# Three small reorderings in a tuned attention and GLU kernel: PSUM tiles of the last output, an earlier tanh, and LayerNorm work behind the output projection

## The chip, the cores and the metric

One core of a Trainium2 chip. The metric is the device time of one execution in microseconds (us). A profile of one execution of each kernel gives the start and end of every instruction; its span is about 1.7 us shorter than the device time. Some executions, over 1.5% above the fastest of their kernel, are marked slow (one of 43 of the kernel before in the rounds of e13: 258.73 us, the fastest 253.67); every ratio below uses fast runs alone, while the medians of rows that name slow runs include them. The kernel before takes 254.48 us (median of three, 254.15 to 256.01).

## The reference, cut to what matters

```python
mod = (silu(c) @ w_mod)            # sa, ca, ga, sb, cb, gb
h = layernorm(x) * (1 + ca) + sa
x = x + ga * A(h)                  # 16 heads of 28, 4 segments of 512 tokens:
                                   # softmax attention inside a segment (a_dot), and
                                   # phi(q) @ M / (phi(q) @ z) from the segments before (a_mem),
                                   # mixed by sigmoid(beta), then @ wo
h = layernorm(x) * (1 + cb) + sb
x = x + gb * B(h)                  # (sigmoid(h @ w_gate) * (h @ w_up)) @ w_down, F = 1792
```

x is 2048 x 448 in bf16. A causal mask acts inside a segment.

## The kernel before

Everything lies in SBUF. TensorE (PE) gets one long list of matmuls; a small clock in the program (`later`, `tick`) decides where the work of the other engines is put into their own lists. PSUM tiles of the tag "m" (q, k, v, `acc`, `mem`, `gps`, `ups`, `dps`, `pwo`) rotate through four buffers. VectorE (DVE) empties most of them, ScalarE (ACT) does exponentials and copies, GpSimd (POOL) masks and `rs`, SyncE (SP) issues transposes through the DMA.

```python
# conditioning: c arrives by DMA; PE multiplies silu(c) with w_mod
    th = const.tile([KP, NK], F32)
    nc.scalar.activation(th[:], c_col[:], AF.Tanh, scale=0.5)
# ... (after the weight loads were issued)
    for t in range(TPS):
        ln0.stats(t)
        if t % 2:
            ln0.rstd(t - 1, t + 1)
    silu_ops()                       # DVE: silu from th
    mod_cols(((1, 1),), warm[:, 2, :])   # PE

class LN:                            # cut
    def rstd(self, a, b):            # POOL: (var + eps) ** -0.5
    def norm(self, i):               # DVE: xn = (x - mean) * rs, and a small copy
    def norm_t(self, i):
        self.norm(i)
        nc.sync.dma_start_transpose(self.h[:, :, i*P:(i+1)*P], self.xn[:, i, :])   # hT, SP's queue
    def modulate(self, kc, vi):      # DVE, on hT

def phi(src, wait, tag, then=None):  # exp on ACT, then two DVE instructions (lines 369, 370)
def mem_read(s, hc):                 # PE: mem; DVE lines 478 to 482 read it and free its PSUM buffer
def pv(s, hc):                       # PE: acc; DVE lines 457 to 463 read it

def wo_fin(s, t):                    # after the Wo matmuls of token tile t
    nc.vector.tensor_tensor(xt, pw[:, 0:D], xt, ALU.add)
    ...
    ln.stats(t)
    ln.rstd(t, t + 1)
    later((2400, 2000, 2000, 1500)[s], lambda: ln.norm_t(t), ("ln2", s))
    # modulate follows once all four tiles are transposed; gate_up reads hT

def down(s, t):
    dp = m_f32("dps")
    ...
    n = 2 if i == NSEG * TPS - 1 else 1      # the very last tile goes in two halves
    for h in range(n):
        c = slice(h * D // n, (h + 1) * D // n)
        for fc in range(NFC):
            nc.tensor.matmul(dp[:, c], ...)
        nc.vector.tensor_tensor(ot[:, c], dp[:, c], x_sb[:, i, c], ALU.add)
        eng.dma_start(out_dram[...], ot[:, c])
```

The softmax here doesn't subtract the row's maximum and nothing guards it: scores larger than these inputs give would overflow.

Of the kernel before, what the change touches and what calls it, by code (L numbers as in the profile page):

```python
# [9 lines left out]
F32 = mybir.dt.float32  # L10
AF = mybir.ActivationFunctionType
# [6 lines left out]
def kernel(  # L18
# [16 lines left out]
    nc = tc.nc  # L35
# [4 lines left out]
    TPS = L // P  # L40
    F = B_w_gate.shape[1]
    NFC = F // P
    KP, NK = 112, 4
# [5 lines left out]
    scale = float(Dh) ** -0.5  # L49
# [10 lines left out]
    const = ctx.enter_context(tc.tile_pool(name="const", bufs=1))  # L60
# [6 lines left out]
    def m_f32(name):  # L67
        return ps_m.tile([P, 512], F32, tag="m", name=name)
# [7 lines left out]
    def later(ns, fn, tag):  # L76
        deferred.append((clock[0] + ns, len(deferred), fn, tag))
# [14 lines left out]
    def need(*tags):  # L92
        for tag in tags:
            late_ = [d for d in deferred if d[3] == tag]
            if late_:
                print("forced", tag, len(late_), max(d[0] for d in late_) - clock[0])
            run_deferred(lambda d: d[3] == tag)


    c_col = const.tile([KP, NK], BF16)  # L100
# [14 lines left out]
    def load_wm(engs, j):  # L115
        t = wm_bufs[j % 2]
        n = NK // len(engs)
        for i, eng in enumerate(engs):
            k = slice(i * n, (i + 1) * n)
            eng.dma_start(t[:, 0:NK * D].rearrange("p (k n) -> p k n", n=D)[:, k, :], wmod_k[:, k, j * D:(j + 1) * D])  # L120
        return t

    wm_bufs = [wts.tile([KP, NK * D + DP - D], BF16, name=f"wm{i}") for i in range(2)]
    wm = {j: load_wm((nc.sync, nc.scalar), j) for j in (1, 0)}
    wq_sb = wts.tile([P, NK, H, HP], BF16)
    wk_sb = wts.tile([P, NK, H, HP], BF16)
    wv_sb = wts.tile([P, NK, D], BF16)
# [64 lines left out]
    coef = const.tile([P, 2, H], F32)  # L192


    th = const.tile([KP, NK], F32)
    nc.scalar.activation(th[:], c_col[:], AF.Tanh, scale=0.5)
    silu = const.tile([KP, NK], BF16)

    def silu_ops():
        nc.vector.tensor_scalar(th[:], th[:], 0.5, 0.5, op0=ALU.mult, op1=ALU.add)  # L200
        nc.vector.tensor_tensor(silu[:], th[:], c_col[:], ALU.mult)
# [13 lines left out]
    def mod_cols(jobs, cp=None):  # L215
        evac = cp is None
        cp = cp_of[0] = m_f32("cp") if evac else cp
        for j, vi in jobs:
            for kc in range(NK):
                for k in range(NK):  # L220
                    c0 = k * D + kc * P
                    if vi >= 2 and kc == NK - 1:
                        for r in (0, LW):
                            nc.tensor.matmul(cp[r:r + LW, vi * NK + kc:vi * NK + kc + 1], lhsT=wm[j][:, c0:c0 + LW],
                                             rhs=silu[:, k:k + 1], start=(k == 0), stop=(k == NK - 1),
                                             tile_position=(0, r))
                        continue
                    nc.tensor.matmul(cp[:, vi * NK + kc:vi * NK + kc + 1], lhsT=wm[j][:, c0:c0 + P],
                                     rhs=silu[:, k:k + 1], start=(k == 0), stop=(k == NK - 1))
        if evac:  # L230
            mod_evac(jobs)
# [281 lines left out]
    def wo_tile(s, t):  # L513
        wo_mm(s, t, range(NK))
        wo_fin(s, t)

    def wo_fin(s, t):
        pw = pw_of.pop(t)
        xt = x_sb[:, s * TPS + t, :]
        nc.vector.tensor_tensor(xt, pw[:, 0:D], xt, ALU.add)  # L520
        if t == 0:
            ln2_of[s] = LN([x_sb[:, s * TPS + i, :] for i in range(TPS)], ("2", s))
        ln = ln2_of[s]
        ln.stats(t)
        ln.rstd(t, t + 1)
        later((2400, 2000, 2000, 1500)[s], lambda: ln.norm_t(t), ("ln2", s))
        if t == TPS - 1:
            for kc in range(NK):
                later(6500 + 400 * kc, lambda kc=kc: ln.modulate(kc, 2), ("ln2", s))
# [33 lines left out]

    def down(s, t):
        need("wd")
        dp = m_f32("dps")
        i = s * TPS + t
        ot = work.tile([P, D], BF16, tag="ot", bufs=2)
        eng = nc.scalar if s >= NSEG - 2 else nc.sync
        n = 2 if i == NSEG * TPS - 1 else 1  # L570
        for h in range(n):
            c = slice(h * D // n, (h + 1) * D // n)
            for fc in range(NFC):
                nc.tensor.matmul(dp[:, c], lhsT=fT_of[(s, fc)][:, t * P:(t + 1) * P], rhs=wd_sb[:, fc, c],  # L574
                                 start=(fc == 0), stop=(fc == NFC - 1))
            nc.vector.tensor_tensor(ot[:, c], dp[:, c], x_sb[:, i, c], ALU.add)  # L576
            eng.dma_start(out_dram[i * P:(i + 1) * P, c], ot[:, c])
# [27 lines left out]
    def down_jobs(s):  # L605
        return [(NFC * MV, lambda t=t: down(s, t)) for t in range(TPS)]
# [66 lines left out]
    for t in range(TPS):  # L673
        ln0.stats(t)
        if t % 2:
            ln0.rstd(t - 1, t + 1)
    silu_ops()
    mod_cols(((1, 1),), warm[:, 2, :])
    for t in range(2):
        ln0.norm(t)  # L680
# [155 lines left out]
    for t in range(TPS):  # L836
        wo_mm(last, t, range(NK - 1 if t < 2 else 0, NK))
        wo_fin(last, t)
        tick((200, 1400, 760, 760)[t])
# [34 lines left out]
```

## Time and profile before

| stretch | where | what PE waits for |
|---|---|---|
| head | 8.62 us | 1.22 us for `silu` |
| segment 0's LN2 | 76.42 us | 1.69 us at `acc`, for a PSUM buffer |
| same | 78.96 us | 0.63 us at the first gate/up, for `hT` |
| tail | 247.50 us | 0.48 us at the last half tile |
| whole | span 252.1 us | PE busy 96% |

In a timeline line the first number is the start and the second the length in us; the bracket at its end is how long the engine idled before it, and for whom. A group of several instructions (x4) is merged into one line. The slice row of the page shows the granted TensorE clock in tenths of full speed, in 40 slices of the span (9 is 90% or more):

```profile
PEclk9999999999999999999999999999999999999999
```

In this execution of the kernel before the clock never fell once it was up.

### The profile page before, as it was taken

How to read it: one execution, taken by the hardware profiler on the slowest of the kernel's cores; microseconds unless marked ns; L12 is line 12 of the kernel's file. 1: busy time of each engine (PE TensorE's matmuls, PEld its weight loads, DVE VectorE, ACT ScalarE, POOL GpSimd, SP SyncE). 2: the span in 40 equal slices, each digit the busy share in tenths (PEclk: the TensorE clock that was granted, in tenths of full speed). 3: DMA queues.
4: the chain of work that ended last, by engine and by line, in shares of the span. 5: the costliest groups of instructions: out<-in, count | busy, mean ns of one | idle time of the engine just before them, and what ended most of it. 6: DMA issues, size and time to landing. Idle time of an engine off the chain costs nothing.

```text
span 252.1 us, 5339 instructions
## 1 busy us (share of the span) xinstructions
PE 242.1 (96%) x2083; PEld 114.4 (45%) x2083; DVE 173.6 (69%) x419; ACT 138.9 (55%) x173; POOL 73.8 (29%) x140
## 2 busy tenths in 40 slices
PE   7899999999987999999999999999999999999994
PEld 3434544446533435545443455454443455333453
DVE  6878799784987776589876756895555585544422
ACT  0468879978896977667285838543642300233200
POOL 4359144223553223334413141471120032000000
PEclk9999999999999999999999999999999999999999
DMA  5999999484034330003342110123110106000011
GB/s 148 290 262 255 349 266 127 86 188 69 3 62 68 62 43 6 19 4 60 79 97 46 22 23 0 25 42 93 45 22 3 21 3 138 18 0 0 3 36 36
DMA packets 41168, 19.66 MB, mean 78 GB/s; under 512 B 30008, under 2 KB 40248, under 8 KB 41144
## 3 DMA queue, kind: packets, MB, share of 16 engines
q1 hardware_dynamic: 38408, 17.61, 32.2%
q10 hardware_dynamic: 2736, 1.72, 2.4%
q8 instruction: 16, 0.26, 0.5%
q14 instruction: 8, 0.07, 0.1%
HBM read 10.67 MB, written 1.84 MB: 50 GB/s over the span
## 4 chain that ended last, share of the span: by engine, by line
PE 52%; DVE 7%; POOL 1%; DMA 1%; ACT 1%; issue 1%; DVEq 0%; POOLq 0%
PE ups L559 13%; PE dps L574 13%; PE gps L542 12%; PE gps L547 5%; PE acc L451 3%; PE pwo L510 2%; PE lg L424 2%; DVE fT L562 1%; DVE st L269 1%; DMA hT<-xn 1%; DVE x_sb L520 1%; DVE ot L576 1%; DVE t L482 1%; PE dM L397 1%; PE ups L547 1%
## 5 line engine op out<-in xcount | busy, mean ns | idle before, releaser
L427 ACT ACTIVATE pT<-lg 128x2048 bf16<-128x2048 f32 (+1 forms) x48 | 76.9, 1602 | 25.9 <-PE lg L424 25.5
L562 DVE SCALAR_TENSOR_TENSOR fT<-tt,ups 128x512 bf16<-128x512 f32 x56 | 37.3, 687 | 39.4 <-PE ups L559 37.5
L437 POOL TENSOR_SCALAR_AFFINE_SELECT pT<-pT 128x512 bf16<-128x512 bf16 x64 | 40.6, 650 | 69.0 <-ACT pT L427 69.0
L550 ACT ACTIVATE tt<-gps 128x512 f32<-128x512 f32 x56 | 30.3, 594 | 55.2 <-PE gps L547 55.2
L574 PE MATMUL dps<-wd_sb,fT 128*128 128x448 bf16 (+1 forms) x238 | 43.9, 341 | 0.5 <-DVE ot L576 0.5
L542 PE MATMUL gps<-hT,wg_sb 128*128 128x512 bf16 x168 | 41.2, 379 | 0.6 <-DVE hT L291 0.6
L559 PE MATMUL ups<-hT,wu_sb 128*128 128x512 bf16 x168 | 41.1, 381 | 0.0
L574 PEld LDWEIGHTS <-fT 128*128 128x128 bf16 x238 | 22.9, 98 | 19.4 <-issue 0.6
L559 PEld LDWEIGHTS <-wu_sb 128*128 128x128 bf16 x168 | 14.1, 98 | 21.7 <-issue 7.9
L542 PEld LDWEIGHTS <-wg_sb 128*128 128x128 bf16 x168 | 15.6, 98 | 18.2 <-DVE hT L291 1.1
L451 PE MATMUL acc<-vt,pT 128*128 128x29 bf16 x640 | 18.5, 175 | 2.1 <-POOL pT L437 1.7
L269 DVE BATCH_NORM_STATS2 st<-x_sb 128x6 f32<-128x448 bf16 x32 | 19.7, 616 | 0.5
L451 PEld LDWEIGHTS <-pT 128*128 128x128 bf16 x640 | 17.6, 96 | 5.2 <-POOL pT L437 2.4
L547 PE MATMUL ups<-hT,wgu_sb 64*128 64x512 bf16 x56 | 17.8, 382 | 0.8 <-ACT tt L550 0.5
L273 POOL TENSOR_SCALAR rs<-mv 128x1 f32<-128x1 f32 (+2 forms) x21 | 5.2, 247 | 44.6 <-DVE mv L270 44.1
L424 PE MATMUL lg<-qT,kT 28*128 28x512 bf16 (+3 forms) x256 | 17.3, 302 | 0.2 <-ACT pT L427 0.2
L547 PE MATMUL gps<-hT,wgu_sb 64*128 64x512 bf16 x56 | 17.0, 381 | 0.0
L343 PE MATMUL pq<-hT,wq_sb 128*128 128x512 bf16 x64 | 16.9, 379 | 0.0
L576 DVE TENSOR_TENSOR ot<-dps,x_sb 128x448 bf16<-128x448 f32 (+1 forms) x17 | 9.9, 590 | 9.6 <-PE dps L574 9.6
L343 PE MATMUL pq<-hT,wk_sb 128*128 128x512 bf16 x64 | 16.4, 379 | 0.0
L277 DVE TENSOR_SCALAR xn<-x_sb,mv,rs 128x448 bf16<-128x448 bf16 x32 | 14.4, 471 | 2.1 <-POOL rs L274 2.0
L274 POOL TENSOR_TENSOR rs<-rs,mhalf 128x1 f32<-128x1 f32 (+2 forms) x21 | 14.2, 678 | 1.7
(101 smaller groups left out, 256.4 us busy)
## 6 DMA issues: line engine op xcount, KB each, us to landing
wm<-in_w_mod_dram SPq DMA_DIRECT2D x4, 392.0 KB, 5.7
x_sb<-in_A_x_dram SPq DMA_DIRECT2D x3, 448.0 KB, 5.4
wd_sb<-in_B_w_down_dram SPq DMA_DIRECT2D x3, 448.0 KB, 9.6
wg_sb<-in_B_w_gate_dram SPq DMA_DIRECT2D x3, 448.0 KB, 9.8
wu_sb<-in_B_w_up_dram SPq DMA_DIRECT2D x3, 448.0 KB, 11.3
out_dram<-ot SPq DMA_DIRECT2D x8, 112.0 KB, 1.8
out_dram<-ot ACTq DMA_DIRECT2D x7, 112.0 KB, 1.7
wm<-in_w_mod_dram SPq DMA_DIRECT2D x2, 196.0 KB
```

What stands on the lines that cost most here:

```text
L269: nc.vector.bn_stats(st[:], self.srcs[i])
L343: nc.tensor.matmul(pq[:, 0:L], lhsT=head_cols(w_sb, k, hc), rhs=h[:, k, :], start=(k == 0), stop=(k == NK - 1))
L424: nc.tensor.matmul(lg[:, hs, wid:wid + nq], lhsT=kT[r, hc, kb * P:(kb + 1) * P], rhs=qT[r, hc, kb * P:L], start=True, stop=True, tile_posi ...
L427: nc.scalar.activation(pT[:, :, w0:w0 + wid], lg[:, :, 0:wid], AF.Exp, scale=scale)
L437: nc.gpsimd.affine_select(out=blk, in_=blk, compare_op=ALU.is_ge, fill=0.0, base=0, pattern=[[0, 4], [1, P]], channel_multiplier=-1)
L451: nc.tensor.matmul(accv[:, qb, hs, 0:ME], lhsT=pT[:, hs, c0:c0 + P], rhs=vt[:, kb, hc * 4 + hs, 0:ME], start=(kb == 0), stop=(kb == qb))
L542: nc.tensor.matmul(g[:, 0:L], lhsT=wg_sb[:, k, f], rhs=h[:, k, :], start=(k == 0), stop=False)
L547: nc.tensor.matmul(dst[:, 0:L], lhsT=wgu_sb[r:r + LW, f], rhs=h[r:r + LW, 3, :], start=first, stop=not first, tile_position=(r, 0))
L550: nc.scalar.activation(tt[:], g[:, 0:L], AF.Tanh, scale=0.5)
L559: nc.tensor.matmul(u[:, 0:L], lhsT=wu_sb[:, k, f], rhs=h[:, k, :], start=False, stop=(k == 2))
L562: nc.vector.scalar_tensor_tensor(ft[:], tt[:], 1.0, u[:, 0:L], op0=ALU.add, op1=ALU.mult)
L574: nc.tensor.matmul(dp[:, c], lhsT=fT_of[(s, fc)][:, t * P:(t + 1) * P], rhs=wd_sb[:, fc, c], start=(fc == 0), stop=(fc == NFC - 1))
```

## The change

Its intent: let the last half tile use its own PSUM buffer; give PE its conditioning operand sooner; and let DVE do the four Wo evacuations and the memory read-out of segment 0 first and the LN2 norms after them, so that PE's PSUM buffers come free sooner. This is all of it:

```diff
     wm = {j: load_wm((nc.sync, nc.scalar), j) for j in (1, 0)}
+    th = const.tile([KP, NK], F32)
+    nc.scalar.activation(th[:], c_col[:], AF.Tanh, scale=0.5)
@@
-    th = const.tile([KP, NK], F32)
-    nc.scalar.activation(th[:], c_col[:], AF.Tanh, scale=0.5)
@@ wo_fin
-        ln.rstd(t, t + 1)
-        later((2400, 2000, 2000, 1500)[s], lambda: ln.norm_t(t), ("ln2", s))
+        if s == 0:
+            later(1800 * (t == TPS - 1), lambda: ln.rstd(t, t + 1), ("ln2", s))
+            later((4000, 3600, 3200, 5000)[t], lambda: ln.norm_t(t), ("ln2", s))
+        else:
+            ln.rstd(t, t + 1)
+            later((2400, 2000, 2000, 1500)[s], lambda: ln.norm_t(t), ("ln2", s))
@@ down
-        dp = m_f32("dps")
         for h in range(n):
             c = slice(h * D // n, (h + 1) * D // n)
+            dp = m_f32("dps")
@@ head
             ln0.rstd(t - 1, t + 1)
-    silu_ops()
+        if t == 1:
+            silu_ops()
```

I call the tail part 1, the tanh part 2 and the norms part 3.

## The prediction

> **What bounds the kernel now.** I read the first page first, then the waits of PE alone, then the timeline in the three stretches that the diff touches. Busy time by engine, from the page:
>
> ```profile
> PE 242.1 (96%) x2083; PEld 114.4 (45%) x2083; DVE 173.6 (69%) x419; ACT 138.9 (55%) x173; POOL 73.8 (29%) x140
> ```
>
> PE is busy 242.1 of 252.1 us, so a change that takes no matmul away can only win what PE idles. The waits of PE alone (engine, what waited, for whom: us in total, times, longest us) name nearly all of that before the last matmul:
>
> ```profile
> PE acc L451 <- POOL pT L437: 1.7, 1, 1.7
> PE warm L647 <- POOL mhalf L167: 1.4, 1, 1.4
> PE warm L228 <- DVE silu L201: 1.2, 1, 1.2
> PE gps L542 <- DVE hT L291: 0.6, 1, 0.6
> PE dps L574 <- DVE ot L576: 0.5, 1, 0.5
> ```
>
> The change aims at four of the five: 1.2 (conditioning), 1.7 + 0.6 (LN2 of segment 0) and 0.5 (last down tile); 4.0 us, 1.6% of the span, is the most it could win. The other is the start.
>
> The tail, in the timeline (start us, length us, engine, line, operation, out<-in):
>
> ```profile
> 247.05 0.39 DVE L576 TENSOR_TENSOR ot<-dps,x_sb 128x224 bf16<-128x224 f32 x1 [0.72 <-PE dps L574]
> 247.50 1.50 PE L574 MATMUL dps<-wd_sb,fT 128*128 128x224 bf16 x14 [0.48 <-DVE ot L576]
> ```
>
> The second half's 14 matmuls start when DVE has read the first half (247.05 + 0.39 = 247.44), though they write other columns: both halves lie in one tile.
>
> The middle, same columns, cut to what matters:
>
> ```profile
> 73.96 2.42 POOL L437 TENSOR_SCALAR_AFFINE_SELECT pT<-pT 128x512 bf16<-128x512 bf16 x4
> 74.03 0.69 DVE L277 TENSOR_SCALAR xn<-x_sb,mv,rs 128x448 bf16<-128x448 bf16 x1 [0.46 <-POOL rs L274]
> ...
> 75.65 0.62 DVE L482 TENSOR_TENSOR t<-mem,r 128x448 bf16<-128x448 f32 x1
> ...
> 76.42 1.15 PE L451 MATMUL acc<-vt,pT 128*128 128x29 bf16 x40 [1.69 <-POOL pT L437]
> ...
> 78.26 1.62 DVE L291 TENSOR_SCALAR hT<-hT,cols 128x512 bf16<-128x512 bf16 x4 [1.21 <-DMA hT<-xn]
> ...
> 78.96 1.66 PE L542 MATMUL gps<-hT,wg_sb 128*128 128x512 bf16 x6 [0.63 <-DVE hT L291]
> ```
>
> The POOL named at 76.42 is not the cause. By the waits in the built program, this acc's first weight load waits for one mask that ended at 70.19, and for DVE's L482, because acc takes the PSUM buffer of that mem tile (four tiles in rotation). L482 ends at 76.27. It is late because four LN2 norms stand before it on DVE, the last of which waited for POOL's rs.
>
> The second wait, 78.96, is for hT: all four transposes must have landed and been modulated. In the SP queue's timeline they are issued at
>
> ```profile
> 69.12 1.19 SPq L287 DMA_TRANSPOSE hT<-xn  x1
> 70.66 1.19 SPq L287 DMA_TRANSPOSE hT<-xn  x1
> 73.30 1.19 SPq L287 DMA_TRANSPOSE hT<-xn  x1
> 75.28 1.20 SPq L287 DMA_TRANSPOSE hT<-xn  x1
> 76.66 1.19 SPq L498 DMA_TRANSPOSE oT<-ou  x1
> ```
>
> Each holds SP for 1.19 us and the median landing is 2.4 us after issue; where four follow each other in this trace (35.41, 36.80, 38.10, 39.41) they are 1.3 us apart. Today they are spread as norms become ready; the last, at 75.28, is ahead of oT.
>
> [...] the xn norm took 0.38 us at 68.49 but 0.69 beside the masks at 74.03. [...]
>
> **The change, part by part.** The build keeps PE's order instruction for instruction; only DVE, POOL, SP and ACT change places.
>
> 1. Separate tiles for the last halves. Nothing is added; the second half starts at about 247.02 instead of 247.50, and its buffer was freed at 241. On the path that sets the end: **-0.48 us**.
>
> 2. Tanh sooner. ACT's table load (1.28 us) and tanh (0.21) move ahead of two wq loads. Before, those loads' own waits held tanh until 7.96. c lands at 4.66, so tanh ends near 4.9, and silu, now behind the second of four stats, near 7.1 instead of 8.56. PE's conditioning matmuls then start at about 7.4 (end of the warm-up), not 8.62. But what follows them is not theirs to give: the transposes need xn of tile 0, which DVE finishes at 8.87 after the same total of stats and silu work as before, and the warm-up matmul between them waits for DVE's cols (end 9.35), again the same sum. Only the later rs and xn move, 0.36 us later (silu's two operations stand before stats 3 and 4): xn of tile 2 ends at 10.23 instead of 9.88, and PE asks for it at 10.44. So **0.0 us**: 1.2 us of wait changes its name. One risk: the DMA semaphores are dealt anew, and the wq pieces k=2 and k=3 now wait for two w_mod halves; the loads that waited for these before were issued at 6.38 and 8.05, against 4.67 and 6.10 for the two wq pieces. They are needed at 11.67 and 12.25; with 4.5 us to landing, as before, k=3 would come at 12.5. But its ACT queue is then empty ahead of it, so I put **+0.1**.
>
> 3. LN2 norms of segment 0. After the change DVE does, from the third tile's aggregate (68.39) on: the acc read-out (1.03 us from 69.00 to 70.03 in the trace), phi of q (0.72, 70.55 to 71.27), the fourth Wo evacuation, and then all four norms. The evacuation starts 0.51 + 0.52 = 1.03 us sooner (two norms with copies gone from before it): 71.27 - 1.03 = 70.24. Add 0.65 + 0.66 + 0.10 (evacuation, stats, aggregate, by start distances): the first norm starts at 71.65 and its copy ends at 72.25, against 69.09 today. I allow 0.2 for phi lying beside masks that POOL now does earlier. The other norms follow at once, with ou between.
>  - acc: the chain to L482 no longer waits for rs behind it; norms 2 to 4 and ou end near 74.4, L482 near 75.5: acc starts at about 75.6 instead of 76.42, 0.8 us sooner.
>  - hT: all transposes are now ready together, and SP is the limit. The built order puts oT between the third and the fourth. Five at 1.31: 72.45, 73.76, 75.07, oT 76.4, the fourth at 77.7; it lands 2.42 later at 80.1, against 77.70. The modulate no longer lies beside masks (before, 0.56 of waiting and 0.65 instead of 0.40), so the first ends near 80.55 and gate/up starts at 80.6 instead of 78.96: **+1.6 us**.
>  PE gets the 0.8 us at acc, and then idles about 3 us before gate/up (acc and four pv matmuls done near 77.6). The wait has moved and grown. PE is dense from there on (its later gaps add up to 1.4 us), so nearly all reaches the end; I take 0.1 as absorbed.
>
> Sum: -0.48 + 0.1 + 1.6 - 0.1 = +1.1 us. 254.48 + 1.1 = **255.6 us**, 0.4% slower.
>
> **Rivals.**
>  (a) It works as meant: acc and gate/up both come sooner, all 4.0 us of waits are at stake and perhaps 2 to 3 come back: about 252. Against: gate/up's weight load waits for all four transposes, and the first cannot be issued before 72.25. For: the author's delays look tuned, and if hT were ready at 78.2 as before, acc's gain would at least not be lost.
>  (b) [...] part of the gate/up work runs at half speed: some 2 us more, about 257.5. [...]
>  (c) The wq pieces land late and the head loses 0.4 us instead of 0.1: 255.9.
>  (d) DVE's backlog clears during PE's idle stretch and later waits of PE (0.31 at 129.48, 0.47 at 142.53) vanish: 254.8.
>
> **Range and chances.** The three runs of before spread over 1.9 us, so the median has some 0.5 us of its own. The first transpose's time (0 to 0.6 late) and (c), (d) give the rest: 254.0 to 257.2. To be faster by 2% takes 249.4, more than all the waits aimed at; slower by 2% is 259.6, (b) with more on top. 1%, 97%, 2%.
>
> **What would show it.** Step 1: the second half's matmuls follow the first within 0.1 us. Step 2: conditioning matmuls near 7.4, but qT's first projection still near 12.77. Step 3: acc near 75.6 with a gap under 1.2 us; SP's transposes 1.3 us apart with oT before the last one; first gate/up near 80.6 after 3 us of idling. I am wrong if gate/up starts before 79.5, if the projection moves by over 0.4 us, or if PE's granted clock dips after the gap.

## The result

The changed kernel takes 258.07 us (median of four, 257.81 to 259.01); the kernel before took 254.45 us in the same rounds (four runs, 254.15 to 256.01). The ratio is 1.0136, 95% interval 1.0088 to 1.0185: slower by 1.4%, still within 2%, but outside the predicted range of 254.0 to 257.2. A ratio here is the mean time of one kernel's fast runs over the mean of the other's fast runs of the same rounds, so not quite the ratio of the medians.

The profiled executions have spans of 252.1 and 256.4 us. Busy time and clock, from the page of the changed kernel:

```profile
PE 243.7 (95%) x2083; PEld 114.8 (45%) x2083; DVE 173.9 (68%) x419; ACT 139.0 (54%) x173; POOL 74.0 (29%) x140
...
PEclk9999999999997799999999999999999999999999
```

PE is busy 1.6 us longer (243.7 against 242.1) with the same 2083 matmuls, and the clock has a dent: 0.50 from 80.03 to 86.86 us. The waits of PE alone:

```profile
PE gps L546 <- DVE hT L291: 3.7, 1, 3.7
PE acc L451 <- DVE t L482: 1.8, 1, 1.8
...
PE lntr L693 <- DVE xn L277: 0.7, 1, 0.7
PE warm L668 <- DMA wd_sb<-in_A_wq_dram: 0.6, 1, 0.6
```

The wait for `silu` is gone, and two others stand in its place (0.7 for the first norm, 0.6 for a piece of wq). The wait at `acc` has not shrunk, and that at gate/up went from 0.63 to 3.7. (Lines behind 122 have moved by up to five: 546 is gate/up, 542 before.) The middle in the timeline:

```profile
69.85 0.77 DVE L369 TENSOR_SCALAR r<-qT 128x512 bf16<-128x512 bf16 x1
70.71 0.68 DVE L370 TENSOR_TENSOR e<-e,r 128x512 bf16<-128x512 bf16 x1
...
72.71 0.38 DVE L277 TENSOR_SCALAR xn<-x_sb,mv,rs 128x448 bf16<-128x448 bf16 x1
...
76.19 0.62 DVE L482 TENSOR_TENSOR t<-mem,r 128x448 bf16<-128x448 f32 x1
...
76.97 1.16 PE L451 MATMUL acc<-vt,pT 128*128 128x29 bf16 x40 [1.83 <-DVE t L482]
...
82.13 1.06 DVE L291 TENSOR_SCALAR hT<-hT,cols 128x512 bf16<-128x512 bf16 x3 [4.59 <-DMA hT<-xn]
...
82.60 2.31 PE L546 MATMUL gps<-hT,wg_sb 128*128 128x512 bf16 x5 [3.71 <-DVE hT L291]
```

The profile itself now names the memory read-out (482) as what `acc` waits for. It ends 0.54 us later than before, not sooner, and the first norm starts only at 72.71. SP's queue:

```profile
73.34 3.82 SPq L287 DMA_TRANSPOSE hT<-xn  x3
...
77.78 1.21 SPq L498 DMA_TRANSPOSE oT<-ou  x1
79.05 1.25 SPq L287 DMA_TRANSPOSE hT<-xn  x1
```

Three transposes stand 1.3 us apart (73.34, 74.65, 75.95); then 0.6 us pass between the end of the third (77.16) and oT. The tail:

```profile
251.97 0.39 DVE L580 TENSOR_TENSOR ot<-dps,x_sb 128x224 bf16<-128x224 f32 x1 [0.72 <-PE dps L578]
253.31 0.39 DVE L580 TENSOR_TENSOR ot<-dps,x_sb 128x224 bf16<-128x224 f32 x1 [0.95 <-PE dps L578]
```

The two last additions are 1.34 us apart; before they started at 247.05 and 249.04, 1.99 apart.

The sum, from the start of the same instruction in both traces: the first gate/up comes 3.64 us later (82.60 against 78.96; 0.34 of it stood already when the third Wo tile was evacuated). From there to a set of logits matmuls later on, 13.14 us of work before (78.96 to 92.10) take 14.48 (82.60 to 97.08): +1.34. From there to the tail nothing much changes (-0.06), and the tail gives -0.65. Together +4.27 us, the start of the last addition (253.31 against 249.04).

### The profile page after: what moved, and what is told of

Same layout as the page of the kernel before. It is cut to its first block, busy times and chain, and to the rows that moved or that the text cites. A ratio compares the mean times of both kernels' runs of the same rounds, so it can differ in the third digit from the quotient of the medians.

```text
span 256.4 us, 5338 instructions
## 1 busy us (share of the span) xinstructions
PE 243.7 (95%) x2083; PEld 114.8 (45%) x2083; DVE 173.9 (68%) x419; ACT 139.0 (54%) x173; POOL 74.0 (29%) x140
## 3 DMA queue, kind: packets, MB, share of 16 engines
q10 hardware_dynamic: 2736, 1.72, 2.4%
## 4 chain that ended last, share of the span: by engine, by line
PE 51%; DVE 7%; POOL 1%; DMA 1%; ACT 1%; issue 1%; DVEq 0%; POOLq 0%
PE ups L563 13%; PE dps L578 12%; PE gps L546 12%; PE gps L551 5%; PE acc L451 3%; PE pwo L510 2%; PE lg L424 2%; DVE fT L566 1%; DVE st L269 1%; DMA hT<-xn 1%; DVE x_sb L520 1%; DVE t L482 1%; PE dM L397 1%; PE ups L551 1%; PE mem L475 1%
## 5 line engine op out<-in xcount | busy, mean ns | idle before, releaser
L546 PE MATMUL gps<-hT,wg_sb 128*128 128x512 bf16 x168 | 42.2, 388 | 3.7 <-DVE hT L291 3.7
```

The lines of the kernel that those rows point to most:

```text
L546: nc.tensor.matmul(g[:, 0:L], lhsT=wg_sb[:, k, f], rhs=h[:, k, :], start=(k == 0), stop=False)
```

## The experiments

### Each part alone

```diff
# e1_tail_only: before + part 1
# e2_tanh_only: before + part 2
# e3_tanh_swap: before + part 2, and
-        other = nc.scalar if w is A_wq else nc.sync
+        other = nc.sync if w is A_wq else nc.scalar
# e4_ln2_only: before + part 3
```

> Part 1 alone (own PSUM tile for each last down half) on the kernel before. Theory (the parts are independent, and the tail's gap of 0.48 us was all on the path): the second half's matmuls follow the first without a gap; span 0.4 to 0.7 us shorter than 252.1, time about -0.5 us. Rival (the gain of the tail in the changed kernel was the longer gap on ACT or DMA moving): less than 0.2 us.

> Part 2 alone (tanh ahead of two wq loads, silu behind the second stats). Theory D (semaphores dealt anew: wq pieces k=2, k=3 issued at 6.6 and 8.3 instead of 4.7 and 6.1, k=3 lands after 12.2): a PE gap of about 0.6 us before the bias matmuls, first qT projection near 13.2 instead of 12.77, time +0.3 to +0.5 us, and from there to the end the same distances as before. Rival T (DVE's reordered stats hold the head): the gap stands before transposes instead, at 9 to 10.5 us, and the bias matmuls wait for nothing. If part 2 is harmless: projection at 12.6, time -0.2 us.

> As the run with part 2 alone, but the wq pieces k=2, k=3 are issued on SP and the wk pieces on ACT (same bytes, other queue). Theory D: wq k=3 lands before 11.8, its gap of 0.57 us is gone; if the wk pieces, now the late ones, land before they are asked for (they are needed 0 to 1 us later), the first qT projection comes at about 12.6 and time is 0.1 to 0.2 us under before; if wk k=3 is late instead, the gap stays at the same bias matmul, which reads both. Rival T: nothing changes against the run with part 2 alone (projection near 13.2).

> Part 3 alone (the four LN2 norms of segment 0 behind the fourth Wo evacuation). Theory (the loss is made in the middle, by itself): first gate/up near 82.2 instead of 78.96 after a PE gap of 3.5 us or more, granted clock at half for about 6.8 us, one minus the other +4.2 to +5 us in span. Rival (it needs the head's delay to trip the clock[...]): gate/up near 82.2 but no half clock, +3.2 us.

| run | median us (runs) | before, same rounds | ratio, 95% interval |
|---|---|---|---|
| e1, part 1 | 254.19 (6) | 254.85 (11) | 0.9967 [0.9943, 0.9991] |
| e2, part 2 | 254.46 (6) | 254.85 | 0.999 [0.9969, 1.0012] |
| e3, part 2, loads swapped | 254.98 (6) | 254.85 | 0.9998 [0.9977, 1.0019] |
| e4, part 3 | 258.9 (4) | 254.85 | 1.0161 [1.013, 1.0193] |

The loss is all in part 3. Part 1 wins what was worked out; its tail in the timeline:

```profile
248.08 0.39 DVE L576 TENSOR_TENSOR ot<-dps,x_sb 128x224 bf16<-128x224 f32 x1 [0.72 <-PE dps L574]
249.42 0.39 DVE L576 TENSOR_TENSOR ot<-dps,x_sb 128x224 bf16<-128x224 f32 x1 [0.95 <-PE dps L574]
```

The distance is 1.34 again. Part 2 alone is a null: in e2 PE has its conditioning operand at 7.41, then idles 0.91 us for the first norm and 0.42 us for the last piece of wq; its first q projection starts at 13.09 (before 12.77) and its first gate/up at 79.19. In e3 the wait for that piece is gone, but the projection still starts at 13.00. In that execution the clock was first up at 7.04 (4.83 in e2), conditioning ran only at 8.50, and the bias matmuls took 1.35 us in place of 1.01. So e3 shows that the late piece is not needed to make part 2 a null, but not what the head would gain without it. Nor is all of that delay part 2's for certain: the first projection starts at 12.95 to 13.23 in the seven traces with part 2 and at 12.74 to 12.93 in those without it (e13 left out, for its six memsets in the head), but once, in e4, at 13.14. Part 3 alone has the changed kernel's middle:

```profile
82.59 1.03 PE L546 MATMUL gps<-hT,wg_sb 128*128 128x512 bf16 x2 [3.38 <-DVE hT L291]
```

Its trace has the clock at half for 10.24 us (78.25 to 88.49), so part 2 is not needed for the clock to fall.

### The clock

The same stretch of work in the windows view of before, the changed kernel and e5 (columns: length, busy time of PE, of its weight loads, DVE, ACT, POOL, then granted clock, DMA share, GB/s). e5 is the changed kernel with dummy matmuls in the gap:

```diff
         gp = [m_f32("gps") for _ in fcs]
+        if s == 0 and f0 == 0:
+            for _ in range(14):
+                nc.tensor.matmul(gp[0][:, 0:L], lhsT=ident[:], rhs=wg_sb[:, 0, 0:L], start=True, stop=True)
```

> The changed kernel with 14 dummy matmuls of 512 columns ahead of segment 0's first gate/up; the true matmul overwrites their result. Clock theory: they only fill the idle 3.7 us (14 x 0.22 = 3.0 us), gate/up still starts within 0.3 of 82.6, no half-clock window follows, the span is 1.0 to 1.7 us shorter than the changed kernel's 256.4 (about 255.0; device about 256.7) and the mean clock is 0.993 or more. Rival (the clock is not the cause; what follows the gap is slow for other reasons): no change, about 258.

Before:

```profile
78.96:92.10 13.14, 12.97 (x112) 5.35 (x113) 10.98 (x30) 10.17 (x13) 2.52 (x4) 1.00 0.28 40
```

Changed:

```profile
82.60:97.08 14.48, 14.33 (x113) 5.54 (x113) 10.98 (x30) 10.17 (x13) 2.52 (x4) 0.85 0.14 29
```

e5:

```profile
83.13:96.26 13.13, 12.97 (x113) 5.32 (x112) 10.98 (x30) 10.18 (x13) 2.53 (x4) 1.00 0.15 32
```

With the gap filled, the work takes 13.13 us again: the 1.34 us are the clock. Yet e5 took 258.25 us (4 runs; before 254.45 in 11; ratio 1.0152 [1.0134, 1.017]), no faster. Two things took the gain back in its profile. The dummies themselves ran at half clock for a while (0.50 from 77.07 to 80.48; 14 from 79.45 on took 3.70 us, not 3.0) and gate/up started 0.53 us later than in the changed kernel, because the fourth transpose held SP for 1.76 us in place of 1.25. And near 175 us a later transpose held SP for 2.05 in place of 1.19; PE then waited twice, and was back at the changed kernel's times by 182.28. Why those two transposes took longer I did not find out. So the clock's 1.34 us are shown, the 1.0 to 1.7 us that I expected from filling the gap are not.

Between the start and the end of a trace, every stretch at half clock is 3.41 us long or a multiple of it (3.41 in e1, 6.83 in the changed kernel and e7, 10.24 in e4). e1 has one of 3.41. Its windows, cut at the edges of that stretch:

```profile
73.95:77.36 3.41, 1.72 (x51) 1.17 (x50) 2.83 (x7) 3.41 (x6) 2.37 (x4) 1.00 0.39 79
77.36:80.77 3.41, 3.41 (x14) 1.14 (x12) 2.51 (x8) 1.09 (x3) 1.23 (x2) 0.50 0.72 82
```

PE was busy for half of a window (1.72 of 3.41 us) and got half clock (0.50) for the whole of the next, though its gap was 1.69 us only. The kernel before has the same gap (1.69 us, PE busy 1.72 us from 73.95 to 77.36, then a clock of 1.00), and of 118 fast runs of it in the timed jobs of e1, e5, e9, e12 and e14, 27 had a mean clock of 0.998 or more (mean 254.31 us), 84 had 0.990 to 0.993 (255.02 us) and 7 less (256.49 us). The profiled execution is not among these, but was of the kind of the 27 (its clock never fell), so the +4.27 us between the two traces overstate the +3.6 us of the medians. The changed kernel's four runs had 0.987, 0.987, 0.98 and 0.987: two or three windows (6.83 us at half clock in its profiled run, of 0.987, and 10.24 in that of e4, of 0.98). Busy time alone does not tell which window drops the clock: windows with 1.57 to 1.92 us of 3.41 were followed by half clock, while one of 1.73 (e14), one of 1.86 (e2) and one of 1.90 (e12) were not. (The clock of these never fell, so their windows are placed by steps of 3.41 us from the moment the clock came up, since in the traces with a drop it begins 71.68 or 75.09 us after that moment, 21 or 22 times 3.413.)

### The norms, the transposes and SP

```diff
# e6_t3_first, on the changed kernel: the fourth transpose of hT goes ahead of oT
-            later((4000, 3600, 3200, 5000)[t], lambda: ln.norm_t(t), ("ln2", s))
+            later((4000, 3600, 3200, 4500)[t], lambda: ln.norm_t(t), ("ln2", s))
# e7_rs_early, on the changed kernel: two of POOL's masks come after rs, not before
-            later(1800 * (t == TPS - 1), lambda: ln.rstd(t, t + 1), ("ln2", s))
+            later(0, lambda: ln.rstd(t, t + 1), ("ln2", s))
```

> The changed kernel with one number changed (5000 to 4500): the fourth transpose of hT goes ahead of oT in SP's order; DVE, POOL and PE keep theirs. Theory (SP's order and its 1.3 us per transpose, with the pause of 0.5 beside oT, are part of the loss): the fourth is issued near 77.2 instead of 79.05, gate/up starts near 80.8, at most one or two half-clock windows; about 256.0 us. Rival (the lateness of DVE's norms is all of it, oT hides beside): gate/up stays within 0.5 of 82.6, about 258.

> The changed kernel with the fourth tile's rs no longer put off: on POOL two of the masks come after it instead of before it; DVE and SP keep their order. Theory (phi of q on DVE is slow, 0.77 + 0.67 instead of 0.28 + 0.43, because POOL masks at the same time): phi is back near 0.72 in all, the first transpose is issued near 72.8 instead of 73.34, gate/up near 82.0; 257.4 us or a little less by the clock. Rival (phi is slow for another reason): phi keeps 1.4 and gate/up stays at 82.6.

e6 took 257.18 us (4 runs; ratio 1.0109 [1.0089, 1.0129], against 1.0152 of e5 and e7 in the same rounds), about 1.0 us less. Gate/up starts at

```profile
81.41 1.03 PE L546 MATMUL gps<-hT,wg_sb 128*128 128x512 bf16 x2 [2.01 <-DVE hT L291]
```

and not at 80.8 as expected: the fourth transpose was issued at 77.78, not 77.2. The 0.5 us pause stands ahead of whatever comes fourth, hT here and oT in the changed kernel. All semaphores that this transpose waits for had been reached long before (the fourth norm's copy ended at 75.90).

e7 took 258.17 us (4 runs; ratio 1.0152 [1.0131, 1.0173]), no better in time. Its DVE timeline at phi of q:

```profile
69.72 0.77 DVE L369 TENSOR_SCALAR r<-qT 128x512 bf16<-128x512 bf16 x1
70.59 0.42 DVE L370 TENSOR_TENSOR e<-e,r 128x512 bf16<-128x512 bf16 x1
```

Line 370 is back at 0.42 where POOL no longer masks, while 369 stays at 0.77 beside the one mask left (69.71 to 70.35). So the masks are what slows phi, 0.26 us of it shown for line 370 and the rest likely for 369. The first transpose came 0.38 us sooner (72.96), 0.12 of which stood already at the first Wo matmul, and gate/up at 82.21. But the fourth norm now lay beside masks (0.77 and 0.49 in place of 0.38 and 0.18) and `acc` came 0.31 later. And gate/up, starting earlier inside the stretch at half clock (80.22 to 87.05), lost 0.29 more to the clock: from it to the same logits matmuls e7 takes 14.77 us, the changed kernel 14.48. So the gain changed places.

### A place in the program

Before the first modulate, DVE passes two waits. The transposes have landed, yet these two are 0.43 us apart in before, e1 and the changed kernel. SP's pause and this one have in common that an 8 KB instruction packet of the DMA follows 0.5 to 0.9 us after each, in the traces of before, the changed kernel, e6, e7 and e8 (at 78.31 and 82.69 in the changed kernel, whose page counts 8 such packets on q14, 0.07 MB). In the kernel before DVE pauses so after its 191st and 447th recorded instruction (0.43 and 0.40 us; after the 319th no pause can be seen); in the runs below with more memsets (e9 to e13) about 0.4 us stand after the 319th instead. These places are 128 apart. SP's pause stands after its 79th recorded instruction in the changed kernel, e4, e5, e7 and e10, whatever comes next. So each pause seems to belong to a place in the program; what makes an engine pause there is not shown, and what is tested is the place alone. To test it, move programs by some places:

```diff
# e9_dve_shift, on e1: one more DVE instruction in the head
     coef = const.tile([P, 2, H], F32)
+    nc.vector.memset(coef[:], 0.0)
# e8_candidate, on e1: one norm of segment 0 goes behind the fourth Wo evacuation
-        later((2400, 2000, 2000, 1500)[s], lambda: ln.norm_t(t), ("ln2", s))
+        later(3000 if s == 0 and t else (2400, 2000, 2000, 1500)[s], lambda: ln.norm_t(t), ("ln2", s))
# e10_cand_shift, on e8: the memset, and the load of beta from nc.sync to nc.scalar
# e11_after_shift, on the changed kernel: the memset, and each of the eight gate/up weight
#   loads on nc.sync in two halves (eight more SP instructions)
# e12_best: e8 with the memset and the split loads
# e13_best_shift6: e12 with six memsets instead of one
# e14_tail_again: e1 once more
```

> The kernel before with part 1 and one norm moved: segment 0's second LN2 norm goes behind the fourth Wo evacuation, where DVE waited 0.46 us for rs. Theory: the fourth evacuation comes 0.5 us sooner, the fourth transpose is issued near 74.8 instead of 75.28 (SP allows it: 72.1 + 2 x 1.3), acc starts near 75.9 and gate/up near 78.45; 0.4 to 0.5 us less than part 1 alone, about 253.8, and the half-clock window may go as well (then 253.1). Rival (SP's queue or the mask engine takes the gain): 254.2, as part 1 alone.

> Part 1 with one tiny extra VectorE memset in the head, so that every later VectorE instruction stands one place further on in its program. Theory: VectorE pauses about 0.43 us [...] (in all traces the two waits just ahead of the first modulate are 0.43 apart, though the transposes have landed, and an 8 KB instruction packet of the DMA follows 0.55 us later); moved by one place, the pause falls into VectorE's idle wait before the landing: modulate starts about 0.1 after the landing (77.8 instead of 78.2), gate/up near 78.45 instead of 78.89, 0.4 us less than part 1 alone (253.8). Rival (the 0.43 belongs to the wait for four transposes, not to the place in the program): nothing moves, 254.2.

> The candidate of e8 with both programs moved: one VectorE memset more in the head, and the load of beta on ScalarE's queue, so SyncE has one instruction fewer before the transposes. Theory (both pauses belong to a place in the program): the fourth transpose is issued 1.3 after the third (75.3 instead of 75.7), the pause comes after it, gate/up starts near 78.4 instead of 79.35, and the whole takes about 1 us less than e8: 254.0, or 253.3 without a half-clock window. Rival (pauses belong to the third transpose in a row and to the wait): gate/up stays at 79.3, 255.0.

> The changed kernel with one VectorE memset more in the head and the eight loads of gate and up weights split in halves (eight more SyncE instructions)[...]. Theory: transposes and oT follow each other 1.3 apart without the 0.5 pause, the fourth is issued near 78.55 instead of 79.05, modulate follows the landing within 0.1; gate/up near 81.7 instead of 82.60, 257.1 us. Of the loss against before, 0.9 us are then these two pauses, which before hid behind the norms or were there as well. Rival: 82.6 and 258.1.

> Part 1, the one moved norm of e8, one VectorE memset more in the head, and the gate and up weight loads split in halves as in e11 [...]. Theory: third and fourth transpose follow 1.3 apart, modulate starts within 0.25 of the landing; the fourth is issued near 75.25, acc near 75.9, gate/up near 78.4 with a gap of about 0.7; 253.7 us, 0.5 below part 1 alone as measured against the kernel before (ratio about 0.995). Rival (what SyncE and VectorE no longer lose there, later waits take back, as in e11): ratio 0.997 to 1.0, as part 1 alone.

> The kernel of e12 with six extra VectorE memsets in the head instead of one. In e12 the last transpose's transfer had 15 of its 16 signals at 77.80 to 77.97 and the last at 78.79: an 8 KB instruction packet (77.35, 0.46 us)[...]. With six, [...] the packet comes near 75.8, before the last transfer (76.7 to 77.6). Theory: the fourth transpose lands 2.4 after its issue at 75.3, gate/up starts near 78.2 instead of 79.45, acc 0.4 later than in e12 (76.4); about 1 us less than e12, 253.7 (ratio 0.995 to 0.997). Rival (the late last signal has another cause and stays with this transfer): gate/up near 79.4, ratio 1.00.

> Part 1 alone once more, to stand on the same chip and rounds as e13: ratio 0.995 to 1.0 as in e1 (0.9967); tail 0.65 us shorter than that of the kernel before.

| run | median us (fast and slow runs) | before, same rounds | ratio, 95% interval |
|---|---|---|---|
| e8 | 254.99 (6) | 254.45 (11) | 1.0024 [0.9999, 1.0049] |
| e9 | 254.66 (22) | 255.0 (27) | 0.9988 [0.9968, 1.0008] |
| e10 | 258.8 (4) | 255.0 | 1.0136 [1.0106, 1.0167] |
| e11 | 258.44 (4) | 255.0 | 1.0134 [1.0098, 1.017] |
| e12 | 255.16 (22, of them 3 slow) | 254.83 (27) | 1.0019 [0.9997, 1.0041] |
| e13 | 255.95 (22) | 254.97 (43, of them 1 slow) | 1.0026 [1.0005, 1.0047] |
| e14 | 254.04 (22) | 254.97 (43, of them 1 slow) | 0.9964 [0.9945, 0.9983] |

**e9** settles DVE's pause. Modulate in the timeline of e1:

```profile
78.19 0.65 DVE L291 TENSOR_SCALAR hT<-hT,cols 128x512 bf16<-128x512 bf16 x1 [1.21 <-DMA hT<-xn]
```

and of e9, where the two waits are 0.08 us apart:

```profile
77.90 1.06 DVE L293 TENSOR_SCALAR hT<-hT,cols 128x512 bf16<-128x512 bf16 x2 [0.84 <-DMA hT<-xn]
```

The last transpose landed at 77.62 in e1 and 77.70 in e9, so one instruction somewhere in the head took 0.37 us out of this wait. In time it is no faster than e1 (the intervals overlap). Its profile has later waits of 0.62 and 0.39 us near 129.5 and 134.9; e1 has 0.46 and 0.40 there, but e14, which is the same kernel as e1, 0.32 and none. The second varies between executions. The first is the pause again: in e9 DVE now idles 0.46 us at 127.56 to 128.02, in the work ahead of the memory read-out that PE waits for there (0.11 at that place in e14). PE's wait there is 0.61 to 0.71 us in the four traces with one memset more (e9 to e12), and 0.29 to 0.46 in the others. So the pause was not removed: it was moved out of one wait of PE and into another, which took back about 0.3 of the 0.37 us (0.62 against 0.32 in e14).

**e11** settles SP's. Its queue, of the changed kernel but for the shift:

```profile
73.08 3.81 SPq L289 DMA_TRANSPOSE hT<-xn  x3
77.08 1.19 SPq L500 DMA_TRANSPOSE oT<-ou  x1
78.32 1.26 SPq L289 DMA_TRANSPOSE hT<-xn  x1
```

oT follows the third transpose 1.40 us after its issue (75.68 to 77.08), where the changed kernel needed 1.83. Gate/up came at 81.54 in place of 82.60; 0.26 of this stood already at the first Wo matmul, about 0.8 are the two pauses. It did not show in the time: with waits of 0.62 and 0.40 us near 134 and 139 (the changed kernel has 0.29 and none) its profiled execution took as long as the changed kernel's (258.12 us). The 1.06 us are accounted for in this trace. Gate/up lost 0.31 more to the clock (14.79 us to the same logits matmuls, not 14.48), and the two waits took 0.73 more (1.02 against 0.29). The first of them is DVE's pause in its new place, as in e9; whether the second came by the shift or by the execution, I can't say.

**e8, e10, e12, e13** were meant to beat e1. In e8 `acc` came at 75.79, as expected, but the fourth transpose at 75.70, later than the 75.28 of before. I had counted from 72.1, where the moved norm starts; its copy ends at 72.6, the transpose is issued at 72.67, and two more at 1.3 us give 75.3 at best, to which SP's pause adds 0.5. In e10 the pause went behind the fourth transpose (issued 1.29 after the third), but the beta load on ACT's queue cost 2.2 us in the head (a 1.44 us gap of PE at 25.33), and the last transfer landed late. The same in e12, which has no cost in the head: the fourth transpose is issued at 75.49, modulate starts only at 78.98. The view of these four transposes in e12, from issue to landing:

```profile
DMA to landing us min/median/max: 2.4/2.4/3.3
```

In e14 it is

```profile
DMA to landing us min/median/max: 2.4/2.4/2.4
```

The last transpose of e12 gave 15 of its 16 signals at 77.80 to 77.97 and the sixteenth at 78.79. An instruction packet lies in that stretch, in the DMA view of e12 from 77 to 78 us (packets, MB, share of 16 engines):

```profile
q14 instruction: 1, 0.01, 2.9%
```

It starts at 77.35 and takes 0.46 us. In e13, with six memsets, the packet comes at 75.95 and another transpose has the late signal: the second of the four (15 signals by 76.56, the last at 77.38). The fourth lands 2.44 us after its issue (76.70 to 79.14), as expected, and modulate follows 0.19 later. So the packet and the late signal moved together in these two, and in e10 as well a packet (79.89) lies near a late last signal (80.99, 15 by 80.07). That the packet holds the signal back is not shown: in the changed kernel a packet at 78.31 lies beside the transfer of oT, which landed 2.43 us after its issue, as usual. The gain was lost all the same: six memsets of DVE in the head held `silu` back until 9.66, and the first projection came at 13.82. From the first Wo matmul to gate/up e13 takes 15.90 us and e14 15.89: with 1.3 us for each transpose, the moved norm has nothing to win.

**e14** repeats part 1 alone: 0.9964, e1 0.9967. It beats the kernel before by 0.35%, and the changed one by 1.7% (0.9965 over 1.0136, so across different rounds), and it is the version to keep.

## Why the prediction was wrong

The class was right (within 2%), the size was not: +3.6 us where the sum said +1.1.

- **Tail, -0.48.** Right. Measured: the last two additions are 0.65 us closer together, and e1 and e14 confirm it in time (0.3% to 0.4%).
- **Head, +0.1.** The mechanism was right (conditioning at 7.46, nothing won, the late piece of wq), the size was not: the first projection came 0.46 us later, and 0.34 were left at the middle. My own rival (c) had 0.4. How much of this is part 2's is not settled (e4 above). Part 2 alone stays a null in time.
- **Middle, +1.6: the step that failed.** It was to start gate/up at 80.6; it started at 82.60. The terms of the difference of 2.0, in order of time: the first transpose at 73.34 instead of 72.45 (0.89: 0.34 of the head, and 0.53 because phi took 1.45 us beside the masks where I had 0.72 and 0.2; e7 shows the masks' part); SP's pause in front of oT (0.46); landing 2.53 instead of 2.42 after issue (0.11); and DVE's 0.43 us between the two waits ahead of modulate, which I had read as masks in its way before, and dropped (0.54 with the rest of the hand-over). e9 and e11 show that both pauses belong to a place in the program (one instruction more on DVE: 0.43 became 0.08; eight more on SP: 1.83 from issue to issue became 1.40). Before, SP's can't be seen; an estimate is that it lay hidden: the wait at its 79th place ended at 74.55, and 0.46 later, at 75.01, the fourth norm (its copy ends at 75.25) was not yet done.
- **acc 0.8 us sooner: wrong in sign.** It came 0.55 later. The read-out was free of the wait for `rs`, but it stood behind a first norm that was about 0.9 later (72.71, where I had 71.65 and 0.2) and a third one beside masks (0.72 and 0.49 for norm and copy, in place of 0.38 and 0.18). So the gap at `acc` stayed at 1.83 us, and gate/up's was added to it.
- **The clock, rival (b).** I put it outside the centre on an assumption of mine that no trace had shown. It cost 1.34 us (14.48 against 13.14 before and 13.13 in e5), and in e1 a window with PE busy for 1.72 of 3.41 us came before a whole one at half clock. It was also not a change from nothing: in most runs of the kernel before the clock is below full too (91 of 118 had a mean of 0.993 or less).
- **Absorbed, -0.1.** Measured -0.06.

Rival (a), both waits shrinking, is out: neither did. So is (d), later waits vanishing: 0.31 and 0.47 us before became 0.29 and 0.47.

## What to carry to other kernels

Work that is put behind other work on one engine moves a whole chain: follow it to the transfer that lands last, and ask what each step lies beside there, since an instruction beside another engine's masks took up to 2.7 times as long (0.77 us in the changed kernel for 0.28 before). A gap of PE can cost more than its length: in the changed kernel the clock fell to half inside the gap of 3.71 us and stayed there until 86.86, which cost 1.34 us more. Compare the granted clock of several runs before believing a gain of 0.5% (in the kernel before, 254.31 us in runs at 0.998 or more, 255.02 at 0.990 to 0.993). Where a gain of some tenths doesn't arrive, look at what it now collides with: several versions here freed a wait and gave it back elsewhere.
